# A fused attention and FFN kernel: rounded and low parts side by side in one 512-column product, a moved write-out and a new repeated order

## The chip, the cores and the metric

The kernel runs on one core of one Trainium2 chip. The metric is the device time of an execution in microseconds. A core has TensorE (PE in the rows; PEld is its weight load), VectorE (DVE), ScalarE (ACT), GpSimd (POOL) and SyncE (SP, which here only issues DMAs). Each engine takes its own instructions in the order in which they stand, and waits for the others through semaphores.

## The reference

Attention with four sink columns and a window of 128 over 4 batches, 8 heads, 768 positions and a head size of 64; its output, laid out as 3072 tokens of 512, goes through an FFN of width 2048 with a hard swish between the layers.

```python
def _attn_ref(q, k, v, n_sink, window):
    scores = (1.0 / np.sqrt(D)) * np.matmul(q, k.transpose(0, 1, 3, 2))
    keep = (pos[None, :] < n_sink) | ((rel >= 0) & (rel < window))   # rel = query - key
    scores = np.where(keep, scores, -1000000000.0)
    a = np.exp(scores - np.max(scores, axis=-1, keepdims=True))
    a = a / (np.sum(a, axis=-1, keepdims=True) + 1e-09)
    return np.matmul(a, v)

def _moe_ref(x, w_in, w_out):          # x (3072, 512), w_in (512, 2048), w_out (2048, 512)
    h = x @ w_in
    g = h * np.clip(h + 3.0, 0.0, 6.0) / 6.0
    return g @ w_out
```

## The kernel before

**Two parts of a number.** An operand is split into a part rounded to the shorter format fp32r and the low part, the difference to the full number. A product then takes three matmuls: rounded x rounded, rounded x low, low x rounded. In the code the names end in h (rounded, high) and l (low): xh, xl, WIH, WIL, gh, g.

**Units and pairs.** The work is cut into 12 units: 4 batches of 3 stretches of 256 positions. A unit has 4 pairs of heads, so there are 48 pairs (s). The first stretches of all batches come first (pairs 0 to 15); the first 10 pairs compute attention in plain fp32.

**Attention of a pair.** `C_score` makes the scores of a head and a tile of 128 queries (c); VectorE reduces them to the row minimum while it writes them to SBUF. `C_soft` does the exponentials (ScalarE), sum and reciprocal (VectorE), an addition of two key blocks (GpSimd) and the scaling (ScalarE, line 331). `D_pt` (d) transposes the weights on TensorE and splits them into ph and pl; GpSimd masks them. `D_snk` (s) does the sink columns. `E_av` (e) multiplies with the values: a head has seven matmuls of 128 or 256 columns, the low ones with 64 output rows. Both heads share one PSUM bank, av. `E_out` joins the two halves in tmp (one ScalarE copy and one VectorE addition a head) and splits the result into xh and xl.

**FFN of a unit.** `ffn1` computes one half (128 of 256 columns of width) of step i: for each of 4 chunks three matmuls of 256 columns, into one half of the bank hps, 12 in all. After both halves ScalarE makes relu(h + 3), VectorE makes min(..., 6) * h, rounds it to gh and takes the low part g. `ffn2` adds that step's share of the second layer for one tile of 128 tokens: six matmuls of 512 columns into o0 or o1. There are 8 steps i; for units from the third on (lag 2) the second layer runs two steps behind the first. `ffn_out` multiplies by 1/6 into SBUF and starts the DMA to the output.

**Order of the work.** A unit's FFN is a queue of 34 places: 16 halves of ffn1, 16 of ffn2 and 2 write-outs. The order in which all instructions are issued is written by hand: a long list for pairs 0 to 15 (FIRST), and then ORDER, repeated for each s; an f in it takes the next place from the FFN queues (`drain`). What remains of the FFN after the last pair is drained at the end. A tile framework puts in the semaphores and gives out the buffers; an instruction whose buffer is still in use is placed later than it is written.

Of the kernel before, what the change touches and what calls it, by code (L numbers as in the profile page):

```python
# [9 lines left out]
F32 = mybir.dt.float32  # L10
# [34 lines left out]
def attn_ffn_kernel(ctx: ExitStack, tc: tile.TileContext, qx, kx, vx, vfx, vsx, n_sink, window, w_in, w_out, out):  # L45
# [248 lines left out]
    PTAGS = [("pl", 2), ("pl", 2), ("Pt", 1)]  # L294

    def cell(s, h, t, c0, c1):

        if plain(s):
            return st_[s][f"P{h}"][:, t * P + c0:t * P + c1]
        return st_[s]["P"][:, h, t * WP + c0:t * WP + c1]  # L300

    def C_score(s, h, t):
# [62 lines left out]
    def D_pt(s, h):  # L365
# [39 lines left out]
    def E_av(s, h):  # L405
# [3 lines left out]
        if h == 0:  # L409
            d["av"] = ps.tile([P, 2, UT], F32, tag="bank", name="av")  # L410
            if not plain(s):
                d["tmp"] = work.tile([P, UT], F32, name="tmp", bufs=1)
        acc = d["av"][:, h, :]

# [4 lines left out]
        if plain(s):  # L419
            pf = d[f"pt{h}"]  # L420
            seq = [(VS[:, slot, h, :], pf[:, c:c + o1 - o0], d["av"][:, 0, o0:o1]) for slot, c, o0, o1 in ops]
        else:

            ph, pl = d[f"pt{h}"]
            vsl = slice(2 * D * h, 2 * D * (h + 1))
            vhi = slice(2 * D * h, 2 * D * h + D)
            high = [(VS[:, slot, vsl], ph[:, c:c + o1 - o0], acc[:, o0:o1]) for slot, c, o0, o1 in ops]
            low = [(VS[:, slot, vhi], pl[:, c:c + o1 - o0], acc[0:D, o0:o1]) for slot, c, o0, o1 in ops]
            seq = [high[0]]
            for a, l in zip(high[1:], low[1:]):  # L430
                seq += [a, l]

            if u:
                seq += [low[0], (sinks[b % 2][:, p, vsl], pz, acc)]
            else:
                seq.append((VS[:, 0, vsl], pl[:, 0:UT], acc))
        for j, (l, r, o) in enumerate(seq):
            nc.tensor.matmul(out=o, lhsT=l, rhs=r, start=(j == 0 and (h == 0 or not plain(s))),
                             stop=(j == len(seq) - 1 and (h == 1 or not plain(s))))
        if h == 1:  # L440
            E_out(s)

    def E_out(s):
        b, u, p = pus[s]
        d = st_[s]
        if p == 0:
            xt[(b, u)] = [None] * NP
        xh = work.tile([P, UT], F32R, tag=f"xh{p}", name=f"xh{p}")
        xl = work.tile([P, UT], F32R, tag=f"xl{p}", name=f"xl{p}")
        xt[(b, u)][p] = (xh, xl)  # L450
        if plain(s):
            acc = d["av"][:, 0, :]
            copy_r(nc, weng(XHF, p), xh, acc)
            nc.vector.tensor_tensor(out=xl, in0=acc, in1=xh.bitcast(F32), op=ALU.subtract)
            return
        tmp = d["tmp"]
        for h, r0, r1 in ((0, slice(0, 64), slice(64, 128)), (1, slice(64, 128), slice(0, 64))):
            acc = d["av"][:, h, :]
            nc.scalar.copy(out=tmp[r0], in_=acc[r1])
            nc.vector.tensor_tensor(out=tmp[r0], in0=acc[r0], in1=tmp[r0], op=ALU.add)  # L460
        copy_r(nc, eng(XHI, s), xh, tmp)
        eng(XLO, s).tensor_tensor(out=xl, in0=tmp, in1=xh.bitcast(F32), op=ALU.subtract)
# [4 lines left out]

    def ffn1(x, i, pool, psum, half, state, tag):

        if half == 0:  # L470
            state["h"] = psum.tile([P, 2, UT], F32, tag=tag or "hps", name="hps")
        hp = state["h"]
        fs = slice(P * half, P * (half + 1))
        n = 3 * NP
        j = 0
        for c in range(NP):
            xh, xl = x[c]
            for l, r in ((WIH[i][:, c, fs], xh), (WIH[i][:, c, fs], xl), (WIL[i][:, c, fs], xh)):
                nc.tensor.matmul(out=hp[:, half, :], lhsT=l, rhs=r, start=(j == 0), stop=(j == n - 1))  # L479
                j += 1  # L480
        if half == 1:
            spare = state["lag"] == 2 and i % 3 == 2
            g = pool.tile([P, 2, UT], F32R, tag="gf" if spare else "g", name="g", bufs=2)
            gh = pool.tile([P, 2, UT], F32R, tag="gf" if spare else "gh", name="gh", bufs=2)
            if state["lag"] == 2:
# [23 lines left out]
    def ffn_out(tt, pool, state, dst):  # L509
        if pool is work:  # L510
            if "o" not in kept:
                kept["o"] = work.tile([P, 2, DM], F32, tag="sb1", name="ost", bufs=1)
            o = kept["o"][:, tt]
# [5 lines left out]
    def ffn_steps(n, x, pool, psum_h, psum_o, dsts, tag=None):  # L519
# [3 lines left out]
        steps = []  # L523
        for i in range(NFP + lag):
# [3 lines left out]
            if i >= lag:  # L528
                for tt in range(2):
                    steps.append((2 * (i - lag + 1), lambda i=i, tt=tt: ffn2(i - lag, tt, psum_o, state, tag)))  # L530
        steps.append((0, lambda: ffn_out(0, pool, state, dsts[0])))
        steps.append((0, lambda: ffn_out(1, pool, state, dsts[1])))
# [267 lines left out]
```

## Time and profile before

| what | value |
|---|---|
| runs shown | 718.99, 717.37, 716.12 us, median 717.37 |
| profiled execution | 716.19 us, its span 714.5 us, granted clock 0.999 |
| TensorE busy | 703.5 us, 4836 matmuls |
| TensorE's weight loads | 640.3 us |
| VectorE busy | 496.0 us |
| ScalarE busy | 413.3 us |
| GpSimd busy | 173.2 us |
| DMA | 89.11 MB, mean 125 GB/s |

The span runs from the first instruction to the last; 1.7 us of the execution's time lie around it. Matmuls overlap: one is printed with some 0.28 or 0.39 us, while the next starts after a shorter time, so what a matmul costs a full TensorE is read from start to start. In the first 170 us the weights are loaded and split, from 170 to 590 the repeated order runs, and from 590 on little but FFN work is left.

### The profile page before, as it was taken

What the parts mean: (1) busy time and instruction counts of PE and PEld (TensorE: products, weight loads), DVE (VectorE), ACT (ScalarE), POOL (GpSimd) and SP (SyncE); (2) the same over time, 40 slices, a digit from 0 to 9 for tenths busy, and PEclk for the clock granted to TensorE, in tenths of its full rate; (3) what the DMA queues carried; (4) which work ended last, traced back from release to release, by engine and by line L of the source; (5) the groups of instructions that cost most, each with busy time, mean ns of one, the idle gap of its engine ahead of it and who ended that gap; (6) DMA issues with size and microseconds to landing.
All of it is one profiled execution on the core that took longest, in us unless ns stands there. A gap on an engine that the chain in (4) does not pass through costs nothing. (4 is left out here: it accounts for less than half of the span.)

```text
span 714.5 us, 14315 instructions
## 1 busy us (share of the span) xinstructions
PE 703.5 (98%) x4836; PEld 640.3 (90%) x4836; DVE 496.0 (69%) x1376; ACT 413.3 (58%) x1080; POOL 173.2 (24%) x336
## 2 busy tenths in 40 slices
PE   9999999999999999999999999999999999999996
PEld 7888888899999999999998998999999899998995
DVE  5999998767777767776777767767776775533331
ACT  6988887676656556556566655655665663311211
POOL 1000000000343333343343343343334344000000
PEclk9999999999999999999999999999999999999999
DMA  8765564555544635545444544553644540000000
GB/s 301 245 216 219 190 198 119 149 132 150 135 103 136 156 103 153 154 104 155 129 111 126 158 111 110 135 150 92 175 129 111 137 99 2 31 1 0 30 1 35
DMA packets 53297, 89.11 MB, mean 125 GB/s; under 512 B 8160, under 2 KB 38112, under 8 KB 51168
## 3 DMA queue, kind: packets, MB, share of 16 engines
q1 hardware_dynamic: 53072, 88.11, 43.6%
q8 instruction: 41, 0.67, 0.4%
q14 instruction: 40, 0.33, 0.1%
q10 hardware_dynamic: 144, 0.00, 0.0%
HBM read 42.47 MB, written 6.29 MB: 68 GB/s over the span
## 5 line engine op out<-in xcount | busy, mean ns | idle before, releaser
L479 PE MATMUL hps<-xh,wih 128*128 128x256 f32 x768 | 219.2, 286 | 0.3 <-DVE tmp L460 0.3
L479 PE MATMUL hps<-xh,wil 128*128 128x256 f32 x768 | 216.6, 282 | 0.0
L479 PE MATMUL hps<-xl,wih 128*128 128x256 f32 x768 | 215.9, 281 | 0.0
L505 PE MATMUL o<-woh,gh 128*128 128x512 f32 x384 | 154.2, 402 | 1.5 <-DVE gh L41 1.5
L505 PE MATMUL o<-woh,g 128*128 128x512 f32 x384 | 151.4, 395 | 0.0
L505 PE MATMUL o<-wol,gh 128*128 128x512 f32 x384 | 151.3, 394 | 0.0
L479 PEld LDWEIGHTS hps<-xh,wih 128*128 128x128 f32 x768 | 144.6, 188 | 2.0 <-PE sp L321 0.5
L479 PEld LDWEIGHTS hps<-xl,wih 128*128 128x128 f32 x768 | 144.8, 188 | 1.2
L479 PEld LDWEIGHTS hps<-xh,wil 128*128 128x128 f32 x768 | 144.6, 188 | 0.1
L492 DVE SCALAR_TENSOR_TENSOR gf<-gf,hps 128x512 f32<-128x512 f32 x96 | 65.7, 685 | 92.8 <-ACT gf L491 92.6
L353 POOL TENSOR_TENSOR Pt<-Pt 128x256 f32<-128x256 f32 x64 | 47.4, 741 | 281.5 <-ACT Pt L345 281.4
L345 ACT ACTIVATE Pt<-Pt,nb 128x272 f32<-128x272 f32 (+2 forms) x152 | 76.9, 506 | 63.3 <-DVE nb L323 62.5
L491 ACT ACTIVATE gf<-hps,three 128x512 f32<-128x512 f32 x96 | 65.9, 687 | 81.2 <-PE hps L479 80.2
L331 ACT ACTIVATE Pt<-Pt,rc 128x144 f32<-128x144 f32 (+2 forms) x152 | 55.3, 414 | 60.4 <-DVE rc L348 36.4
L505 PEld LDWEIGHTS o<-woh,g 128*128 128x128 f32 x384 | 72.2, 188 | 17.3 <-issue 0.3
L505 PEld LDWEIGHTS o<-woh,gh 128*128 128x128 f32 x384 | 72.3, 188 | 11.8 <-ACT gf L491 1.9
L505 PEld LDWEIGHTS o<-wol,gh 128*128 128x128 f32 x384 | 72.4, 189 | 10.3
L494 DVE TENSOR_TENSOR g<-gf,gh 128x512 fp32r<-128x512 f32 x96 | 69.8, 727 | 1.1
L321 PE MATMUL sp<-K 128*128 128x272 f32 (+2 forms) x304 | 60.8, 288 | 1.1 <-DVE pl L30 0.5
L323 DVE CUSTOM_DVE_ANT_0 Pt<-sp,m_t 128x272 f32<-128x272 f32 x128 | 53.8, 428 | 8.3 <-PE sp L321 8.0
L389 POOL TENSOR_SCALAR_AFFINE_SELECT ph<-ph 128x256 fp32r<-128x256 f32 x64 | 30.6, 478 | 117.2 <-ACT ph L35 117.2
L321 PEld LDWEIGHTS sp<-K 128*128 128x128 f32 x304 | 50.3, 188 | 7.8 <-DVE pl L30 0.7
(94 smaller groups left out, 1082.8 us busy)
## 6 DMA issues: line engine op xcount, KB each, us to landing
K<-kt SPq DMA_DIRECT2D x128, 200.0 KB, 3.5
K<-kt SPq DMA_DIRECT2D x152, 64.0 KB, 2.5
st<-in_w_in_dram SPq DMA_DIRECT2D x8, 1024.0 KB, 5.2
st<-in_w_out_dram SPq DMA_DIRECT2D x8, 1024.0 KB, 5.1
kr<-in_kx_dram SPq DMA_DIRECT2D x32, 200.0 KB, 2.4
qr<-in_qx_dram SPq DMA_DIRECT2D x48, 128.0 KB, 2.3
out_dram<-ost SPq DMA_DIRECT2D x24, 256.0 KB, 2.2
vr<-in_vx_dram SPq DMA_DIRECT2D x32, 192.0 KB, 2.5
```

What stands on the lines that cost most here:

```text
L321: nc.tensor.matmul(out=sp[:, 0:w], lhsT=Q[:, h, t * P:(t + 1) * P], rhs=K[:, h, part, k0c:k0c + w], start=(part == 0), stop=(part == 1))
L323: d["min"] = nc.vector.tensor_tensor_reduce(out=cell(s, h, t, 0, w), in0=sp[:, 0:w], in1=m[:, 0:w], scale=-SCALE, scalar=3.0e38, op0=ALU.a ...
L331: nc.scalar.mul(out=blk, in_=blk, mul=c)
L345: d["exp"] = nc.scalar.activation(out=blk, in_=blk, func=AF.Exp, scale=-1.0, bias=nb[:, i:i + 1], accum_out=sm[:, i:i + 1])
L353: nc.gpsimd.tensor_tensor(out=both, in0=both, in1=prior, op=ALU.add)
L389: nc.gpsimd.affine_select(out=prior[i], in_=own[i], pattern=[[0, 2], [-1, P]], base=0, channel_multiplier=1, compare_op=ALU.is_gt, fill=0.0)
L479: nc.tensor.matmul(out=hp[:, half, :], lhsT=l, rhs=r, start=(j == 0), stop=(j == n - 1))
L491: nc.scalar.activation(out=gf, in_=hp, func=AF.Relu, bias=three, scale=1.0)
L492: nc.vector.scalar_tensor_tensor(out=gf, in0=gf, scalar=6.0, in1=hp, op0=ALU.min, op1=ALU.mult)
L494: eng(GLO, state["n"] * NP).tensor_tensor(out=g, in0=gf, in1=gh.bitcast(F32), op=ALU.subtract)
L505: nc.tensor.matmul(out=acc, lhsT=l[:, f, ts_], rhs=r[i][:, f, :], start=(i == 0 and f == 0 and j == 0), stop=(i == NFP - 1 and f == 1 and ...
```

## The change

`ffn1` (units from the third on) multiplies the rounded first-layer weights with xh and xl side by side, as one matmul of 512 columns into both halves of a bank; the low weights still take xh alone. The two results stand beside each other and have to be added: ScalarE copies the second to SBUF (hs), VectorE adds the first. Each half now has a bank of its own, and min and product read h from SBUF. hs lies in the same allocation as the write-out's rows (`spare_rows`, named ost in the rows). `E_av` does the same with ph and pl, in one tile for both, so a head has four matmuls, a bank of its own, and one ScalarE copy and two VectorE additions. Tiles x and ph/pl hold both parts; the plain pairs use one tile for both heads. The write-out is called right after the last `ffn2` of its tile, so a unit's queue has 32 places. ORDER is new.

```diff
-    PTAGS = [("pl", 2), ("pl", 2), ("Pt", 1)]
@@ C_score
-        if t == 0 and plain(s):
-            tag, bufs = PTAGS[(2 * s + h) % len(PTAGS)]
-            d[f"P{h}"] = work.tile([P, 3 * P], F32, tag=tag, name="Ph", bufs=bufs)
+        if i == 0 and plain(s):
+            d["P"] = work.tile([P, 2, 3 * P], F32, tag=("Pt", "ph0")[s % 2], name="Ph", bufs=1)
@@ D_pt
-            ph = work.tile([P, 512], F32, tag="ph", name="pf")
+            if h == 0:
+                d["pf"] = work.tile([P, 2, 512], F32, tag="ph1", name="pf", bufs=1)
+            ph = d["pf"][:, h, :]
...
-        ph = work.tile([P, 512], F32R, name="ph")
-        pl = work.tile([P, 512], F32R, name="pl")
-        d[f"pt{h}"] = (ph, pl)
+        both = work.tile([P, 2, 512], F32R, tag=f"ph{h}", name="ph", bufs=1)
+        ph, pl = both[:, 0, :], both[:, 1, :]
+        d[f"pt{h}"] = both
@@ E_av
-            high = [(VS[:, slot, vsl], ph[:, c:c + o1 - o0], acc[:, o0:o1]) for slot, c, o0, o1 in ops]
-            low = [(VS[:, slot, vhi], pl[:, c:c + o1 - o0], acc[0:D, o0:o1]) for slot, c, o0, o1 in ops]
...
+        av = ps.tile([P, 2, UT], F32, tag="bank", name="av")
+        vsl = slice(2 * D * h, 2 * D * (h + 1))
+        seq = [(VS[:, slot, vsl], d[f"pt{h}"][:, :, c:c + o1 - o0], av[:, :, o0:o1]) for slot, c, o0, o1 in ops]
+        if u:
+            seq.append((sinks[b % 2][:, p, vsl], pz, av[:, 0, :]))
...
+        rows = d["tmp"][D * h:D * (h + 1)]
+        nc.scalar.copy(out=rows, in_=av[D:P, 0, :])
+        nc.vector.tensor_tensor(out=rows, in0=av[0:D, 1, :], in1=rows, op=ALU.add)
+        nc.vector.tensor_tensor(out=rows, in0=av[0:D, 0, :], in1=rows, op=ALU.add)
@@ ffn1
+    def spare_rows():
+        if "sb1" not in kept:
+            kept["sb1"] = work.tile([P, 4, DM], F32, tag="sb1", name="ost", bufs=1)
+        return kept["sb1"]
...
-        for c in range(NP):
-            xh, xl = x[c]
-            for l, r in ((WIH[i][:, c, fs], xh), (WIH[i][:, c, fs], xl), (WIL[i][:, c, fs], xh)):
-                nc.tensor.matmul(out=hp[:, half, :], lhsT=l, rhs=r, start=(j == 0), stop=(j == n - 1))
+        lag2 = state["lag"] == 2
+        if lag2:
+            hp = psum.tile([P, 2, UT], F32, tag=tag, name="hps")
+            for c in range(NP):
+                nc.tensor.matmul(out=hp, lhsT=WIH[i][:, c, fs], rhs=x[c], start=(c == 0), stop=False)
+                nc.tensor.matmul(out=hp[:, 0, :], lhsT=WIL[i][:, c, fs], rhs=x[c][:, 0, :],
+                                 start=False, stop=(c == NP - 1))
+            hs = spare_rows()[:, 2 + i % 2].rearrange("p (a b) -> p a b", a=2)
+            nc.scalar.copy(out=hs[:, half, :], in_=hp[:, 1, :])
+            nc.vector.tensor_tensor(out=hs[:, half, :], in0=hp[:, 0, :], in1=hs[:, half, :], op=ALU.add)
+            hp = hs
@@ ffn_steps
+        def second(i, tt):
+            ffn2(i, tt, psum_o, state, tag)
+            if i == NFP - 1:
+                ffn_out(tt, pool, state, dsts[tt])
...
-        steps.append((0, lambda: ffn_out(0, pool, state, dsts[0])))
-        steps.append((0, lambda: ffn_out(1, pool, state, dsts[1])))
@@ the repeated order
-    ORDER = "v c00 f c01 f c10 f c11 e0 l f k e1 f q f d0 f d1 s f"
+    ORDER = "f f c00 c01 c10 k e0 f q c11 e1 f f l v d0 f f d1 f s"
```

On TensorE, the first two chunks of a half of ffn1, in before (x chunks with their weights, into the bank hps):

```order
L479 MATMUL hps<-xh_4882,wih_110 128x256
L479 MATMUL hps<-xl_4883,wih_110 128x256
L479 MATMUL hps<-xh_4882,wil_118 128x256
L479 MATMUL hps<-xh_5077,wih_110 128x256
L479 MATMUL hps<-xl_5078,wih_110 128x256
L479 MATMUL hps<-xh_5077,wil_118 128x256
```

and the whole half after the change:

```order
L467 MATMUL hps<-x_4754,wih_113 128x512
L468 MATMUL hps<-x_4754,wil_121 128x256
L467 MATMUL hps<-x_4937,wih_113 128x512
L468 MATMUL hps<-x_4937,wil_121 128x256
L467 MATMUL hps<-x_5124,wih_113 128x512
L468 MATMUL hps<-x_5124,wil_121 128x256
L467 MATMUL hps<-x_5313,wih_113 128x512
L468 MATMUL hps<-x_5313,wil_121 128x256
```

Six rows for two chunks became four, with the same number of columns.

On TensorE, the values of one head of a later stretch in before (ph, pl: the two parts of the weights; pz, vs: the sinks):

```order
L438 MATMUL av<-ph,VS 128x256
L438 MATMUL av<-ph,VS 128x128
L438 MATMUL av<-pl,VS 64x128
L438 MATMUL av<-ph,VS 128x128
L438 MATMUL av<-pl,VS 64x128
L438 MATMUL av<-pl,VS 64x256
L438 MATMUL av<-pz,vs 128x256
```

and after the change, with the scores in front of it and the second layer behind it:

```order
L319 MATMUL sp<-K 128x272 x6
L432 MATMUL av<-ph,VS 128x512
L432 MATMUL av<-ph,VS 128x2x128 x2
L432 MATMUL av<-pz,vs 128x256
L507 MATMUL o_5923<-woh_126,gh 128x512
```

Seven matmuls became four, two of which write two runs of 128 columns; and three score groups of two matmuls now stand together ahead of the first head's values.

On VectorE, in before, from a head's scores to the reciprocal of its sums (ISA is the reduction of scores, its second row the read of the minimum; gf, gh and g are the FFN's, sm and rc the sums and reciprocals):

```order
L323 ISA Pt,nb<-sp,m_t_101 128x272
L323 ISA nb 128x1
L323 ISA Pt,nb<-sp,m_t_102 128x272
L323 ISA nb 128x1
L492 SCALAR_TENSOR_TENSOR gf<-gf,hps 128x512
L347 TENSOR_SCALAR sm<-sm 128x2
L41 CAST gh<-gf 128x512
L348 RECIPROCAL rc<-sm 128x2
```

and after the change:

```order
L321 ISA Pt,nb<-sp,m_t_101 128x272
L321 ISA nb 128x1
L494 SCALAR_TENSOR_TENSOR gf<-gf,ost 128x512
L321 ISA Pt,nb<-sp,m_t_102 128x272
L321 ISA nb 128x1
L41 CAST gh<-gf 128x512
L321 ISA Pt,nb<-sp,m_t_101 128x272
L321 ISA nb 128x1
L496 TENSOR_TENSOR g<-gf,gh 128x512
L345 TENSOR_SCALAR sm<-sm 128x2
L435 TENSOR_TENSOR tmp<-av,tmp 64x256
L346 RECIPROCAL rc<-sm 128x2
```

Between the second score and the reciprocal there now stand one more score, the low part g and one of the new value additions.

## Rows read from the trace of the kernel before

**Rows 1.** The page: busy us of each engine; granted clock in 40 slices.
```profile
PE 703.5 (98%) x4836; PEld 640.3 (90%) x4836; DVE 496.0 (69%) x1376; ACT 413.3 (58%) x1080; POOL 173.2 (24%) x336
...
PEclk9999999999999999999999999999999999999999
```

**Rows 2.** Waits of TensorE: engine, line, releaser: us in total, times, longest.
```profile
PE o L505 <- DVE gh L41: 1.5, 1, 1.5
```

**Rows 3.** Timeline of TensorE near the end: start us, us, engine, line, operation.
```profile
608.57 0.34 PE L438 MATMUL av<-ph,VS 128*128 128x256 f32 x2
...
609.22 0.40 PE L505 MATMUL o<-woh,gh 128*128 128x512 f32 x1
...
611.26 0.40 PE L505 MATMUL o<-woh,gh 128*128 128x512 f32 x1
...
618.24 0.28 PE L479 MATMUL hps<-xh,wih 128*128 128x256 f32 x1
...
626.78 0.39 PE L505 MATMUL o<-woh,gh 128*128 128x512 f32 x1
```

**Rows 4.** Windows: stretch, its us, busy us of each engine (instructions), clock, DMA.
```profile
170.00:590.00 420.00, 419.24 (x2944) 385.91 (x2944) 308.91 (x889) 255.36 (x725) 162.92 (x306) 1.00 0.49 128
590.00:714.50 124.50, 118.51 (x757) 106.67 (x755) 45.32 (x97) 23.64 (x48) 7.29 (x15) 1.00 0.04 14
```

**Rows 5.** Groups by form: count | busy us, mean ns of one | idle before.
```profile
L494 DVE TENSOR_TENSOR g<-gf,gh 128x512 fp32r<-128x512 f32 x96 | 69.8, 727 | 1.1
L492 DVE SCALAR_TENSOR_TENSOR gf<-gf,hps 128x512 f32<-128x512 f32 x96 | 65.7, 685 | 92.8 <-ACT gf L491 92.6
L460 DVE TENSOR_TENSOR tmp<-av,tmp 64x256 f32<-64x256 f32 x76 | 31.9, 420 | 13.9 <-ACT tmp L459 13.3
L30 DVE TENSOR_TENSOR pl<-pt,ph 128x256 fp32r<-128x256 f32 x64 | 26.5, 419 | 7.3 <-ACT ph L35 6.2
L35 ACT ACTIVATE ph<-pt 128x256 fp32r<-128x256 f32 x64 | 24.2, 383 | 21.7 <-PE pt L371 21.3
```

**Rows 6.** Timelines of TensorE, VectorE and ScalarE in one repeated pass.
```profile
302.54 0.38 PE L371 MATMUL pt<-ident_r,Pt 128*128 128x128 f32 x2
...
307.60 0.41 PE L321 MATMUL sp<-K 128*128 128x272 f32 x2
307.85 0.39 PE L505 MATMUL o<-woh,gh 128*128 128x512 f32 x1
...
316.67 0.38 PE L371 MATMUL pt<-ident_r,Pt 128*128 128x128 f32 x2
...
305.19 0.42 DVE L30 TENSOR_TENSOR pl<-pt,ph 128x256 fp32r<-128x256 f32 x1
305.52 0.68 DVE L494 TENSOR_TENSOR g<-gf,gh 128x512 fp32r<-128x512 f32 x1
...
309.62 0.69 DVE L492 SCALAR_TENSOR_TENSOR gf<-gf,hps 128x512 f32<-128x512 f32 x1 [1.10 <-ACT gf L491]
...
311.43 0.72 ACT L331 ACTIVATE Pt<-Pt,rc 128x144 f32<-128x144 f32 x2 [1.34 <-DVE rc L348]
```

**Rows 7.** Timeline of TensorE: values of two first-tile heads; split products of a later one.
```profile
130.85 0.41 PE L438 MATMUL av<-ph,VS 128*128 128x256 f32 x2 [0.15 <-DVE gf L492]
...
131.33 0.39 PE L505 MATMUL o<-woh,gh 128*128 128x512 f32 x1
...
313.46 0.28 PE L438 MATMUL av<-ph,VS 128*128 128x128 f32 x1
313.57 0.34 PE L438 MATMUL av<-pl,VS 128*64 128x128 f32 x2
```

**Rows 8.** Timeline of ScalarE at the end of the run.
```profile
707.19 0.60 ACT L516 ACTIVATE ost<-o 128x512 f32<-128x512 f32 x1 [6.33 <-PE o L505]
...
708.59 0.60 ACT L516 ACTIVATE ost<-o 128x512 f32<-128x512 f32 x1 [0.81 <-PEq L646]
```

**Rows 9.** The page, DMA issues: count, KB each, median us to landing.
```profile
K<-kt SPq DMA_DIRECT2D x128, 200.0 KB, 3.5
```

More of the change, by code (lines that the diff above doesn't have):

```diff
@@ L408, in E_av @@
         VS = d["VS"]
[L409 to L413, printed above, removed]
         if u:
@@ L437, in E_av @@
-        for j, (l, r, o) in enumerate(seq):
-            nc.tensor.matmul(out=o, lhsT=l, rhs=r, start=(j == 0 and (h == 0 or not plain(s))),
-                             stop=(j == len(seq) - 1 and (h == 1 or not plain(s))))
+            if h == 0:
+                d["av"] = ps.tile([P, UT], F32, tag="bank", name="av")
+            pf = d["pf"][:, h, :]
+            seq = [(VS[:, slot, h, :], pf[:, c:c + o1 - o0], d["av"][:, o0:o1]) for slot, c, o0, o1 in ops]
+            for j, (l, r, o) in enumerate(seq):
+                nc.tensor.matmul(out=o, lhsT=l, rhs=r, start=(j == 0 and h == 0), stop=(j == len(seq) - 1 and h == 1))
@@ new lines, in E_av @@
+            if h == 1:
+                split_x(s, d["av"])
+            return
+        if h == 0:
+            d["tmp"] = work.tile([P, UT], F32, name="tmp", bufs=1)
+        av = ps.tile([P, 2, UT], F32, tag="bank", name="av")
[3 more added lines that the diff above has]
+            seq.append((sinks[b % 2][:, p, vsl], pz, av[:, 0, :]))
+        for j, (l, r, o) in enumerate(seq):
+            nc.tensor.matmul(out=o, lhsT=l, rhs=r, start=(j == 0), stop=(j == len(seq) - 1))
@@ L440, in E_av, with split_x @@
+        rows = d["tmp"][D * h:D * (h + 1)]
+        nc.scalar.copy(out=rows, in_=av[D:P, 0, :])
+        nc.vector.tensor_tensor(out=rows, in0=av[0:D, 1, :], in1=rows, op=ALU.add)
+        nc.vector.tensor_tensor(out=rows, in0=av[0:D, 0, :], in1=rows, op=ALU.add)
         if h == 1:
-            E_out(s)
-    def E_out(s):
+            split_x(s, d["tmp"])
+    def split_x(s, src):
         b, u, p = pus[s]
-        d = st_[s]
         if p == 0:
             xt[(b, u)] = [None] * NP
[L448 to L462, printed above, removed]
@@ L465, in attn_ffn_kernel @@
+        xb = work.tile([P, 2, UT], F32R, tag=f"x{p}", name=f"x{p}")
+        xt[(b, u)][p] = xb
+        hi, lo = (weng(XHF, p), nc.vector) if plain(s) else (eng(XHI, s), eng(XLO, s))
+        copy_r(nc, hi, xb[:, 0, :], src)
+        lo.tensor_tensor(out=xb[:, 1, :], in0=src, in1=xb[:, 0, :].bitcast(F32), op=ALU.subtract)
     LAG2 = 2
     kept = {}
+    def spare_rows():
+        if "sb1" not in kept:
+            kept["sb1"] = work.tile([P, 4, DM], F32, tag="sb1", name="ost", bufs=1)
+        return kept["sb1"]
@@ new lines, in ffn1 @@
+        if lag2:
[8 more added lines that the diff above has]
+            hp = hs
+        else:
+            if half == 0:
+                state["h"] = psum.tile([P, 2, UT], F32, tag=tag or "hps", name="hps")
+            hp = state["h"]
+            for c in range(NP):
+                xh, xl = x[c][:, 0, :], x[c][:, 1, :]
+                for j, (l, r) in enumerate(((WIH, xh), (WIH, xl), (WIL, xh))):
+                    nc.tensor.matmul(out=hp[:, half, :], lhsT=l[i][:, c, fs], rhs=r,
+                                     start=(c == 0 and j == 0), stop=(c == NP - 1 and j == 2))
@@ L510, in ffn_out @@
         if pool is work:
-            if "o" not in kept:
-                kept["o"] = work.tile([P, 2, DM], F32, tag="sb1", name="ost", bufs=1)
-            o = kept["o"][:, tt]
+            o = spare_rows()[:, tt]
         else:
```

34 lines of the change are left out of this document (7 added, 27 removed).

## The prediction

> **What bounds the kernel now.** I read the page's busy table first, then the waits of TensorE, its timeline for the spacing of products, the windows, and last the chain of one softmax. TensorE is busy for 703.5 of 714.5 us, at full granted clock (the 2.4 GHz level) in all 40 slices [rows 1]. Ends of matmuls are modelled, so that share alone proves little; the waits do: the longest total of its own is 1.5 us, a single wait [rows 2]. TensorE is fed, and the time is the sum of what its products occupy. What one occupies is the distance from its start to the next start, not its printed duration. In the FFN work near the end, 30 products of 512 columns stand between 611.26 and 618.24 (0.2327 us each) and 72 of 256 columns between 618.24 and 626.78 (0.1186 each) [rows 3]. Two of 256 take 0.2372, which is 0.0045 us more than one of 512: columns cost nearly the same, an instruction a few ns. That is the whole lever of the first half of this change.
>
> VectorE is busy for 308.9 and ScalarE for 255.4 of the 420 us from 170 to 590, the stretch of repeated passes (74% and 61%); from 590 on both are mostly idle [rows 4].
>
> **The change part by part.**
>
> *First layer of the FFN.* Ten of the twelve units (from the third on) are altered. Each has 8 steps of 2 halves with 4 chunks, so 640 pairs of 256-column products become one product of 512; the product with the low weights stays. 640 x 0.0045 = 2.9 us off TensorE. The ends I keep are 0 (a pair costs what the wide one does) and 5 us (8 ns a pair).
>
> Added: 160 copies of 128x256 out of PSUM on ScalarE and 160 additions of 128x256 on VectorE. The nearest rows are the ScalarE copy of 128x256 from PSUM, 383 ns, and the VectorE subtraction of 128x256 with one operand in PSUM, 419 ns [rows 5]; I take these: 61 us on ScalarE, 67 us on VectorE in all. From below, a VectorE operation of this size holds up the next one for 0.33 us only (305.19 to 305.52 [rows 6]), which makes 53 us; from above stand the 685 ns of an operation of twice the columns [rows 5], 110 us. The product min(...)*h now reads its second operand in SBUF instead of PSUM: between the 685 ns it takes now and the 727 ns of the low part of g, which has both in SBUF [rows 5]; at 80 calls at most 3 us of VectorE. None of this is on TensorE; what hides it is worked out below.
>
> *Values.* A head of a later tile pair had seven products, from 608.57 to 609.22, 0.65 us [rows 3]. It now has one of 512 columns and three of 256: 0.2327 + 3 x 0.1186 = 0.589. So 0.061 less, for 64 heads 3.9 us. The twelve heads of first tiles that are not in plain fp32 go from four products to two, 0.351 us by the same spacing; before, four of them lie between 130.85 and 131.33, 0.48 us, behind a wait of 0.15 [rows 7]: 0 to 0.13 saved, I take 0.06, 0.7 us in all. Two of the four new products of such a head, and one of the two of a first tile, write two runs of 128 columns with a gap between. No product of before shows that. From below they cost what 256 columns cost, 0.119; from above, what two products of 128 columns cost, up to 0.11 each (313.46 to 313.57 [rows 7]), so 0.22. I take 0.119, since the column count is the same; the upper end is 140 x 0.10 = 14 us.
>
> On this the Trainium skill speaks against the change: its page "PSUM — Partial Sum Buffer", Specifications (TRN2), says that any non-contiguous access pattern slows matmuls significantly, with lines of 8 bytes. No row here shows such a write; each run of these is 512 bytes long, which is why the rule gets a small chance below.
>
> VectorE gets 76 more additions of 64x256 at 420 ns [rows 5], 32 us.
>
> *Write-out.* The two write-out steps of a unit were places in the queue without a product; now the same ScalarE multiply and DMA follow the unit's last products. At the end of the run nothing moves: the first half's multiply already starts at 707.19, beside the other half's products, and the last one at 708.59 behind the last product [rows 8]. Each of the eight FFN places of a pass now carries products, so attention is spread over more FFN work and the tail gets shorter: a shift, zero in the sum.
>
> *New order.* Three of the four score groups and the first value group stand together, and FFN steps in pairs. Neither has a price on TensorE in the old passes. The keys' step stands one score earlier, but its DMAs write the single K buffer, so they are still held until the fourth score has read it; the larger of them take 3.5 us to land [rows 9], and the next pass's first score comes some 11 us after that score. SP's loads behind them are for later passes. Zero, and if that cover were gone the wait would show as TensorE waiting on DMA.
>
> *Buffers of the plain start.* The first ten pairs share fewer buffers; the written-out start is otherwise the same. Zero, 2 us either way.
>
> **Sum.** 2.9 + 3.9 + 0.7 = 7.5 us. The profiled execution has a span of 714.5 and a time of 716.19, so 1.7 lie around it; its new time would be 708.7. The median of the runs shown, 717.37, lies 1.2 above it and would become 709.9. I say 709.
>
> **What hides the additions.** A pass (one pair of heads) lasts 14.1 us on TensorE, from the transposes at 302.54 to those at 316.67 [rows 6]. VectorE at 74% has some 10.4 us in it. It gains four FFN additions and two value additions, 2.5 us by durations, 2.0 by starts: 12.4 to 12.9 of 14.0 us, and 1.1 to 1.6 us are left. ScalarE goes from 8.6 to 10.1. Capacity is there; the question is the order of arrival. In before, from the second score (307.60) to the end of the scaled weights (311.43 + 0.72 = 312.15) the softmax of a head takes 4.55 us, and its transposes come at 316.67 only [rows 6]. In the new order there stand between them two scores of 0.25 (307.60 to 307.85), two value groups of 0.59, one second-layer step and two first-layer halves of 1.40 each: 5.9 us, with the second score's own 0.25 6.1. VectorE's queue now holds one more score, one low part of g and one value addition ahead of the reciprocal: 0.43 + 0.73 + 0.42 by durations, about 1.3 us by starts. If all of that adds, the chain takes 5.85 of 6.1 us; but in the old chain VectorE was idle for 1.10 us before its product at 309.62 [rows 6], and part of the added work falls in there. So the slack is 0.25 to 1.5 us: enough, but here the change can fail.
>
> **Rivals.**
>
> A, forecast: TensorE stays the bound and saves its 7.5 us. Its own range is 705 to 713. Chance 0.62.
>
> B, the other side: the scaled weights of the first head come too late, the transposes wait in each of the 32 full passes, and as TensorE takes its products in order, the FFN products queued behind wait with them. For it: VectorE at 88 to 92%, and that slack. Against it: the idle 1.10 us; and the second layer runs two steps behind the first, so it has several us before it needs g. It decides from 0.23 us a pass (7.5 / 32), where the gain is gone; at 0.5 us a pass the time is 709 + 16 = 725. Chance 0.11.
>
> C, the same wait at about 0.25 us a pass, or in some passes only: 709 + 8 = 717, no change. Chance 0.15.
>
> D, the split writes of the values cost as two products each: 709 + 14 = 723. Chance 0.05. This is what the rule of the Trainium skill's PSUM page would do here.
>
> E, the wide product gives nothing, since a column costs the same in either form: only the values gain, 4.6 us, 712. For it: the difference is 4.5 ns in 237. Chance 0.07. On this the Trainium skill's page "TensorE: Matmul & The Clock Gate", Back-to-back issue gap, gives N/2.4 + 2.5 ns per product, so an estimate of 2.5 ns a pair and 1.6 us in all; its sustained 131 ns for 512 columns in the same section does not fit this trace, which has 232.7.
>
> **Numbers.** A measurement of this kernel can tell about 0.5% from no change: 713.8 to 721.0 is the same. Faster: A and most of E, 0.68. Same: C and a little of E and B, 0.18. Slower: the rest of B and D, 0.14. The range is 704 to 718: it holds A, C and E, and B and D lie above it.
>
> **What would show it.** In the profile after: a first-layer half with eight products in 1.40 us instead of 1.42; a head's values in 0.59. VectorE busy near 595 us and ScalarE near 475, where the page of before has 496 and 413 [rows 1]. Starts of the products with two runs 0.12 apart confirm the price, 0.2 is D. Waits of TensorE that stay under some 3 us in total say A; a wait of the transposes on ScalarE that comes back in each pass says B or C. The forecast is wrong if the products' spacing shrinks as said but the sum of TensorE's waits grows by 7 us or more.

## The result, and the profile after

The changed kernel takes 708.16 us (median of 4 runs, 706.12 to 709.82), the kernel before 716.75 beside it (median of 4). The ratio is 0.9877, 95% interval [0.9834, 0.992]; a second set of runs (below) gave 0.9892 [0.9869, 0.9915]. The forecast was 709 in 704 to 718. The profiled execution took 709.82 us, its span 708.1.

The page of after, busy us of each engine:

```profile
PE 695.5 (98%) x3980; PEld 601.0 (85%) x3980; DVE 578.7 (82%) x1612; ACT 474.2 (67%) x1240; POOL 197.1 (28%) x336
```

TensorE has 856 matmuls fewer than in [rows 1] (640 pairs, 64 x 3 in the values of later tiles, 12 x 2 of first tiles). VectorE and ScalarE carry the new work, and GpSimd, whose instructions are the same, takes 24 us more.

Windows of after (the columns of [rows 4]):

```profile
170.00:590.00 420.00, 420.00 (x2326) 362.51 (x2325) 371.27 (x1065) 299.05 (x834) 177.79 (x291) 1.00 0.49 126
590.00:708.10 118.10, 112.12 (x573) 94.22 (x572) 65.53 (x161) 45.24 (x112) 16.38 (x29) 1.00 0.11 33
```

In the repeated passes VectorE went from 74% to 88%, and TensorE still has no gap: 420.00 of 420.00 us. Its own waits, the three largest by total:

```profile
PE pt L369 <- ACT Ph L329: 2.3, 1, 2.3
PE idle L86 <- POOL rel L65: 1.2, 1, 1.2
PE o L507 <- DVE gh L41: 1.1, 1, 1.1
```

Each is one single wait, as in [rows 2], and none lies between 190 and 600 us, where no product and no weight load of TensorE waits for `Pt`, the weights of later pairs. Spacing of products, timeline of TensorE in after:

```profile
613.07 0.63 PE L432 MATMUL av<-ph,VS 128*128 128x512 f32 x3
613.53 0.28 PE L432 MATMUL av<-pz,vs 128*128 128x256 f32 x1
613.65 0.39 PE L467 MATMUL hps<-x,wih 128*128 128x512 f32 x1
...
657.20 0.40 PE L467 MATMUL hps<-x,wih 128*128 128x512 f32 x1
...
665.61 0.39 PE L507 MATMUL o<-woh,gh 128*128 128x512 f32 x1
```

A head's values take 0.58 (613.07 to 613.65), where [rows 3] had 0.65. Six halves of the first layer with 48 products stand between 657.20 and 665.61: 1.402 each, where the 72 products of [rows 3] took 1.423.

One pass of after, from sink product to sink product, with the softmax that can stop it (TensorE, then ScalarE):

```profile
400.57 0.22 PE L400 MATMUL spt<-ident_r,ssc 128*128 128x128 f32 x1
...
409.90 0.38 PE L369 MATMUL pt<-ident_r,Pt 128*128 128x128 f32 x2
...
414.52 0.22 PE L400 MATMUL spt<-ident_r,ssc 128*128 128x128 f32 x1
...
408.93 0.72 ACT L329 ACTIVATE Pt<-Pt,rc 128x144 f32<-128x144 f32 x2 [0.65 <-DVE rc L346]
```

The pass lasts 13.95 us (14.13 in [rows 6]). The scaled weights end at 409.65, and their transposes start at 409.90: a slack of 0.25 us by this measure, the lower end of what was forecast.

**Pass lengths.** A pass can be read to 0.05 us from the start of one sink product to the next, far finer than the time of a run: two profiled executions of the changed kernel whose spans are 2.5 us apart both have a mean of 13.922. This table is worked out from those starts, 31 passes in each kernel, the mean without the first three and the last two:

```
kernel                                       usual pass      longer ones                     mean
changed                                      13.87 to 13.95  none but the last (14.35)       13.92
old first layer                              13.95 to 14.11  none                            14.02
new order and write-out alone                14.05 to 14.20  none                            14.12
old order                                    13.85 to 13.95  3 of 14.04 to 14.08             13.89
old values, joined together                  14.01 to 14.04  22 of 14.59 to 14.92            14.59
old values, joined head by head              14.00 to 14.04  14 of 14.31 to 15.14            14.31
 the same, row minimum ahead of the product  13.99 to 14.11  4 of 14.21 to 14.33             14.07
low part of g twice                          -               13.95 to 15.08, 23 of 14.4 on    14.62
transposes together                          13.88 to 13.93  7 of 14.54 to 14.62, last 14.40 14.09
 the same, first values later                13.88 to 13.93  none                            13.90
```

### The profile page after: what moved, and what is told of

The parts are those of the page before. It is cut to its first block, busy times and chain, and to the rows that moved or that the text cites. A ratio compares the mean times of both kernels' runs of the same rounds, so it can differ in the third digit from the quotient of the medians.

```text
span 708.1 us, 13020 instructions
## 1 busy us (share of the span) xinstructions
PE 695.5 (98%) x3980; PEld 601.0 (85%) x3980; DVE 578.7 (82%) x1612; ACT 474.2 (67%) x1240; POOL 197.1 (28%) x336
## 4 chain that ended last, share of the span: by engine, by line
PE 89%; DMA 3%; ACT 3%; DVE 2%; SPq 1%; issue 1%; ACTq 0%; DVEq 0%
PE o L507 36%; PE hps L467 21%; PE hps L468 11%; PE av L432 6%; PE sp L319 5%; PE hps L481 4%; PE pt L369 3%; DMA st<-in_w_in_dram 2%; PE av L419 1%; PE idle L86 1%; PE sp L314 1%; SPq L271 1%; DMA K<-kt 1%; DMA raw<-in_n_sink_dram 1%; ACT st L163 1%
## 5 line engine op out<-in xcount | busy, mean ns | idle before, releaser
L467 PE MATMUL hps<-x,wih 128*128 128x512 f32 x640 | 233.3, 400 | 0.0
L468 PE MATMUL hps<-x,wil 128*128 128x256 f32 x640 | 180.4, 282 | 0.0
L351 POOL TENSOR_TENSOR Pt<-Pt 128x256 f32<-128x256 f32 x64 | 57.6, 900 | 345.7 <-ACT Pt L343 345.7
L467 PEld LDWEIGHTS hps<-x,wih 128*128 128x128 f32 x640 | 120.5, 188 | 23.3
L468 PEld LDWEIGHTS hps<-x,wil 128*128 128x128 f32 x640 | 120.7, 189 | 0.4
L493 ACT ACTIVATE gf<-ost,three 128x512 f32<-128x512 f32 x80 | 57.8, 723 | 61.4 <-DVE ost L472 61.4
L471 ACT COPY ost<-hps 128x256 f32<-128x256 f32 x160 | 58.1, 369 | 57.8 <-PE hps L468 56.1
L472 DVE TENSOR_TENSOR ost<-hps,ost 128x256 f32<-128x256 f32 x160 | 66.5, 416 | 31.8 <-ACT ost L471 31.3
L389 POOL TENSOR_SCALAR_AFFINE_SELECT ph<-ph 128x256 fp32r<-128x256 f32 x128 | 74.0, 579 | 53.9 <-ACT ph L35 53.9
L507 PEld LDWEIGHTS o<-woh,gh 128*128 128x128 f32 x384 | 72.4, 188 | 14.7 <-ACT gf L493 1.4
L507 PEld LDWEIGHTS o<-wol,gh 128*128 128x128 f32 x384 | 72.6, 189 | 11.9
L494 DVE SCALAR_TENSOR_TENSOR gf<-gf,ost 128x512 f32<-128x512 f32 x80 | 55.7, 697 | 22.2 <-ACT gf L493 19.6
L391 POOL TENSOR_SCALAR_AFFINE_SELECT ph<-ph 128x256 fp32r<-128x256 f32 x128 | 66.5, 522 | 26.1 <-DVE ph L30 18.5
```

Of the source, the lines that this page charges most:

```text
L351: nc.gpsimd.tensor_tensor(out=both, in0=both, in1=prior, op=ALU.add)
L389: nc.gpsimd.affine_select(out=prior[i], in_=own[i], pattern=[[0, 2], [-1, P]], base=0, channel_multiplier=1, compare_op=ALU.is_gt, fill=0.0)
L391: nc.gpsimd.affine_select(out=own[i], in_=own[i], pattern=[[0, 2], [1, P]], base=0, channel_multiplier=-1, compare_op=ALU.is_ge, fill=0.0)
L467: nc.tensor.matmul(out=hp, lhsT=WIH[i][:, c, fs], rhs=x[c], start=(c == 0), stop=False)
L468: nc.tensor.matmul(out=hp[:, 0, :], lhsT=WIL[i][:, c, fs], rhs=x[c][:, 0, :], start=False, stop=(c == NP - 1))
L471: nc.scalar.copy(out=hs[:, half, :], in_=hp[:, 1, :])
```

## The experiments

Theory: TensorE stays fed, and the gain is the sum of smaller products. Rivals: the new order or the write-out made it; the softmax's slack is used up; VectorE's total, not its order, is what limits.

**The changed kernel again.** No edit.

> The changed kernel once more, on the chip and beside the runs of the next three. Every theory: a ratio to before of 0.986 to 0.991.

708.29 us (704.96 to 712.30, 6 runs), ratio 0.9892 [0.9869, 0.9915]. The gain holds in a second set of runs. The runs scatter over 7 us, those of before beside them over 3 (714.35 to 717.32, 17 runs); more on that below.

**Old first layer.** Three products of 256 columns a chunk, no additions.

```
-        if lag2:
+        if False:
             hp = psum.tile([P, 2, UT], F32, tag=tag, name="hps")
```

> The changed kernel with its first layer as before (three products of 256 columns a chunk into one bank for both halves, no copy and no addition), the rest changed. Theory (the gain is the sum of fewer products on TensorE): 2.9 to 3.8 us slower than the changed kernel, so a ratio to before of about 0.992; first-layer halves 1.42 us instead of 1.40; VectorE busy falls by some 67 us and that gains nothing. Rival (the gain is the new order and write-out, the products are worth nothing): the ratio stays at 0.988. Rival (the additions on VectorE cost time): faster than the changed kernel, ratio under 0.986.

709.51 us (708.02 to 710.57), 0.9916 [0.9903, 0.9929]. Its passes are 0.097 us longer than those of the changed kernel, 3.0 us over 31 passes. By the ratio alone (0.0024 apart, intervals that overlap) the first layer's part would not be told from nothing; by the pass it is.

**New order and joined write-out alone,** on the kernel before.

```
-    ORDER = "v c00 f c01 f c10 f c11 e0 l f k e1 f q f d0 f d1 s f"
+    ORDER = "f f c00 c01 c10 k e0 f q c11 e1 f f l v d0 f f d1 f s"
...
+        def second(i, tt):
+            ffn2(i, tt, psum_o, state, tag)
+            if i == NFP - 1:
+                ffn_out(tt, pool, state, dsts[tt])
```

> The kernel before with only the new repeated order and the write-out joined to the last step; products as before. Theory: 0 on TensorE, ratio 0.998 to 1.002. Rival (the gain is order and write-out): 0.988 to 0.992.

713.43 us (12 runs), 0.9978 [0.9969, 0.9987]: 1.6 us, a small gain and not quite zero. In before TensorE's products wait three times between 190 and 600 us (twice for keys, `K<-kt`, 0.5 us in all, once 0.3 us for the joining); here none does. From here to the old first layer only the values (and buffers) differ: 0.097 us a pass again.

**Old order** in the changed kernel (the ORDER line above, the other way round).

> The changed kernel with the old repeated order. Theory: the order is worth nothing on TensorE as long as it is fed; the old order leaves the first head more time between its scores and its transposes but packs the second one closer, so a ratio of 0.988 to 0.991 to before and waits of TensorE under 5 us more. Rival (the added work on VectorE is only hidden because of the new order): TensorE waits for scores or transposes in each pass, 0.3 us or more a pass, ratio 1.0 or above.

708.77 us, 0.991 [0.9896, 0.9925], against 0.9892 with the new order: no difference that can be told, and its passes are no longer (13.89 against 13.92). The order is not what made the gain.

**Old values.** Seven products a head, both heads in one bank, joined after the second.

```
+            d["av"] = ps.tile([P, 2, UT], F32, tag="bank", name="av")
...
+        for x, l in zip(high[1:], low[1:]):
+            seq += [x, l]
...
+            for g, r0, r1 in ((0, slice(0, 64), slice(64, 128)), (1, slice(64, 128), slice(0, 64))):
+                nc.scalar.copy(out=d["tmp"][r0], in_=acc[r1])
+                nc.vector.tensor_tensor(out=d["tmp"][r0], in0=acc[r0], in1=d["tmp"][r0], op=ALU.add)
```

> The changed kernel with the values' products as before (seven a head, one bank for both heads, one addition a head), the rest changed. Theory: 4.6 us slower than the changed kernel, ratio to before about 0.994; a head's values 0.65 us instead of 0.59; VectorE busy some 32 us less. Rival (order and write-out): 0.988. Rival (VectorE's additions cost time): under 0.986.

729.23 us, 1.0199 [1.0176, 1.0222]: the forecast of 0.994 failed by 18 us. Only some passes have the 14.02 us that the products add up to. VectorE had less to do (340.7 us of the 420) than in the changed kernel (371.3), so it isn't its total. TensorE's weight loads wait between 190 and 600 us for the softmax and, less, for GpSimd's masks:

```profile
PEld pt L369 <- ACT Pt L329: 10.7, 26, 0.8
PEld av L441 <- POOL ph L391: 5.3, 7, 0.8
```

**Old values, joined head by head.** The same products, a bank for each head, copy and addition right behind each.

```
+        acc = ps.tile([P, UT], F32, tag="bank", name="av")
...
+        nc.scalar.copy(out=rows, in_=acc[D:P])
+        nc.vector.tensor_tensor(out=rows, in0=acc[0:D], in1=rows, op=ALU.add)
```

> The changed kernel with the values' seven products a head as before, but each head in a bank of its own and joined right after its products, as in the changed kernel (one addition a head instead of two). Theory (the run with the old values lost its time because both heads were joined only after the second, which filled ScalarE and VectorE just ahead of the second softmax, not because of the products): no waits in the passes, 4 to 4.6 us slower than the changed kernel, ratio about 0.994. Rival (the products or the low ones with 64 output rows cost far more in the new order): again 1.01 to 1.02.

720.45 us, 1.0069 [1.0054, 1.0085]. Neither range came (0.994, or 1.01 to 1.02): half of the loss against 0.994 is gone, and 14 of 31 passes are still long. Timelines of the longest, 15.14 us, TensorE, VectorE, ScalarE:

```profile
421.93 0.66 PE L319 MATMUL sp<-K 128*128 128x272 f32 x4
...
429.31 0.62 PE L369 MATMUL pt<-ident_r,Pt 128*128 128x128 f32 x2
429.69 0.48 PE L514 MATMUL o<-woh,gh 128*128 128x512 f32 x1
...
424.11 0.41 DVE L479 TENSOR_TENSOR ost<-hps,ost 128x256 f32<-128x256 f32 x1
425.31 0.69 DVE L501 SCALAR_TENSOR_TENSOR gf<-gf,ost 128x512 f32<-128x512 f32 x1 [0.79 <-ACT gf L500]
425.92 0.43 DVE L321 CUSTOM_DVE_ANT_0 Pt<-sp,m_t 128x272 f32<-128x272 f32 x1
...
428.83 0.72 ACT L329 ACTIVATE Pt<-Pt,rc 128x144 f32<-128x144 f32 x2 [0.17 <-POOL Pt L351]
```

The first score starts at 421.93, and VectorE takes its row minimum at 425.92 only. Right ahead of it stands the FFN product min(...)*h, for which VectorE waits 0.79 us with nothing to do, because its operand comes from ScalarE; wait and product take 1.4 of the 4.0 us, work queued earlier the rest. The scaled weights end at 429.55, and the second transpose waits for them. In the changed kernel the row minimum stands ahead of that product in the same place, 0.9 us behind its score, which starts at 417.4:

```profile
418.34 0.44 DVE L321 CUSTOM_DVE_ANT_0 Pt<-sp,m_t 128x272 f32<-128x272 f32 x1
419.20 0.69 DVE L494 SCALAR_TENSOR_TENSOR gf<-gf,ost 128x512 f32<-128x512 f32 x1 [0.41 <-ACT gf L493]
```

ORDER writes the product first in both kernels: it belongs to the f ahead of c00. In the changed kernel the framework placed it behind the row minimum in every pass but the last, here it kept the written order in most. Why a change in the values moved it is not shown. The place alone doesn't tell a long pass either: 16 short passes have the product first too, and in 7 of the 14 long ones the row minimum comes first. So the next edit, and not this timeline, is the evidence.

**Row minimum ahead of the product,** the two kernels above with this alone altered: min(...)*h, gh and g of a pass's first step are held back.

```
+            if kept.get("hold"):
+                late.append(product)
...
+                if step == "c00":
+                    with tc.issue_after(st_[at]["min"].ins):
+                        for product in late:
+                            product()
```

> The kernel with the values' old seven products, joined head by head (1.0069 before), with one thing altered: in the repeated order VectorE takes the FFN product min(...)*h of the pass's first step only behind the first score's row minimum. In the run without this, passes in which that product (which waits for ScalarE) stood ahead of the row minimum took 14.5 to 15.1 us, and the others 14.02 to 14.04. Theory, VectorE's queue: all passes become 14.0 to 14.1 us, some 8 us less in all, ratio 0.994 to 0.997. Rival, the seven products themselves make the next step late (their bank or GpSimd's masks): passes of 14.5 us and more stay, ratio 1.004 to 1.009.

712.63 us, 0.9962 [0.9941, 0.9984]: the passes fall to a mean of 14.07, as the theory had it, those with the row minimum first among them; four of 14.21 to 14.33 us are left. The sorting of passes in this expectation (product first 14.5 to 15.1 us, the others 14.02 to 14.04) is wrong, as said above; what it forecast came all the same. VectorE in a pass of 14.31 us, at the same place of its unit as the one above:

```profile
307.15 0.41 DVE L480 TENSOR_TENSOR ost<-hps,ost 128x256 f32<-128x256 f32 x1
307.49 0.42 DVE L321 CUSTOM_DVE_ANT_0 Pt<-sp,m_t 128x272 f32<-128x272 f32 x1
...
308.35 0.69 DVE L505 SCALAR_TENSOR_TENSOR gf<-gf,ost 128x512 f32<-128x512 f32 x1 [0.43 <-ACT gf L501]
308.96 0.43 DVE L321 CUSTOM_DVE_ANT_0 Pt<-sp,m_t 128x272 f32<-128x272 f32 x1
```

> The same alteration for the kernel with the old values in one bank for both heads (1.0199 before; passes of 14.02 us and of 14.6 to 14.9). Theory, VectorE's queue: the transposes' waits go, passes near 14.05 us, ratio 0.994 to 0.998; where GpSimd's masks stay late for the values behind the old joining of both heads, up to 1.005. Rival, the shared bank or the joining of both heads behind the second head is what makes the passes long: they stay, ratio 1.015 or more.

727.52 us, 1.0172 [1.0152, 1.0192]: here the rival holds. With both heads joined behind the second one, 22 passes stay long whichever stands first, and in them VectorE takes the first row minimum some 4.8 to 5.5 us into the pass (3.5 to 4.4 in the changed kernel). So there are two causes: how the heads are joined (1.0172 against 0.9962; the shared bank and the later joining are not told apart), and the place of one step's FFN work in VectorE's queue (1.0069 against 0.9962).

**Low part of g twice.** VectorE takes the low part of g a second time, 1.2 us more a pass.

```
+            if lag2:
+                eng(GLO, state["n"] * NP).tensor_tensor(out=g, in0=gf, in1=gh.bitcast(F32), op=ALU.subtract)
```

> The changed kernel with the low part g computed twice in the units from the third on: two more VectorE operations of 0.7 us a pass, 0.6 us each from start to start. VectorE has about 1.6 us idle in a pass of 13.9. Theory (the slack of the first head's softmax, 0.3 us in the tightest passes of the trace, is the limit, not VectorE's capacity): TensorE waits for the transposes, 0.2 to 0.6 us in some passes, 5 to 20 us in all, ratio 0.995 to 1.015. Rival (capacity is the limit): 1.2 of 1.6 us fit, ratio as the changed kernel's, 0.986 to 0.991.

728.69 us, 1.0183 [1.0168, 1.0198]. VectorE is busy for 393.9 of 420 us and has room left, yet the time grows by 20 us, 0.70 a pass, a little more than the theory's range. The waits between 190 and 600 us stand with TensorE's weight load, since the transposed block is what it loads:

```profile
PEld pt L369 <- ACT Pt L329: 23.0, 69, 0.9
```

This is the mechanism of the prediction's rival B: 1.2 us more in VectorE's queue, counted by starts, meet a slack of 0.20 to 1.18 us, and what the slack does not take is paid, in some passes more and in some less (13.95 to 15.08 us).

**Transposes together.** Both heads' transposes at the end of the pass, one switch less on TensorE.

```
+    ORDER = "f f c00 c01 c10 k e0 f q c11 e1 f f l v f f d0 d1 f s"
```

> The changed kernel with the transposes of the two heads one behind the other (the step d0 moved behind the next two FFN steps). In the trace of the changed kernel the product behind a pair of transposes starts 0.31 us later instead of 0.23, twice a pass; once of it goes. Theory: 0.083 us x 32 passes, 2.7 us faster than the changed kernel, ratio about 0.984, and more slack for the first head. Rival (GpSimd's masks of both heads then come in one block and the next pass's values wait for them): waits of the values on GpSimd, ratio 0.99 or above.

711.65 us (12 runs), 0.9957 [0.9943, 0.9971]: slower than the changed kernel, where 0.984 was expected. The only waits of TensorE's products between 190 and 600 us, and one of them:

```profile
PE av L432 <- POOL ph L391: 2.8, 7, 0.4
...
305.17 0.74 PE L432 MATMUL av<-ph,VS 128*128 128x512 f32 x3 [0.41 <-POOL ph L391]
```

Every fourth pass the first head's values wait for GpSimd's masks, the first of which now starts 1.2 to 2.6 us later in the pass. The switch saved hardly brings anything: the passes without a wait are 13.88 to 13.93 us, 0.02 less in the mean than the changed kernel's, where 0.083 was expected.

**The same, first values one step later.**

```
+    ORDER = "f f c00 c01 c10 k f e0 q c11 e1 f f l v f f d0 d1 f s"
```

> The changed kernel with both heads' transposes together at the end of the pass (0.9957 before, passes of 13.88 to 13.92 us and every fourth one of 14.54 to 14.62, in which the first head's values waited for GpSimd's masks), and with the first head's values one FFN step later in the next pass. Theory, GpSimd's masks are what made that fourth pass long: it falls to 13.9 us, 0.65 us x 8 = 5 us less, ratio 0.987 to 0.990, no more than the changed kernel gains. Rival, the values' lateness moves on to their joining and the softmax behind it on VectorE and ScalarE: some passes of 14.3 us and more stay, ratio 0.993 to 0.998.

708.51 us (705.10 to 713.28), 0.9921 [0.9891, 0.9951]. The long passes are gone (all 13.88 to 13.93), so the masks were their cause. The ratio lies above the 0.987 to 0.990 of the theory, but the interval is too wide to rank this kernel beside the changed one, and a pass 0.02 us shorter is worth 0.7 us.

**Weights behind the first attention.** ScalarE's first copy of FFN weights, which waits for a DMA, behind the first pair's scaling.

```
+            d["copied"] = copy_r(nc, {"D": nc.vector, "A": nc.scalar}[PFE[h]], ph[:, 0:w], pt[:, 0:w])
...
+                if after == 0:
+                    behind.enter_context(tc.issue_after(st_[0]["copied"].ins))
```

> The changed kernel with one thing altered in its start: ScalarE takes its first copy of FFN weights, which waits for a DMA, only behind the first pair's scaling and copies. In two profiled executions of the changed kernel (spans 708.1 and 710.6 us) that copy waited 2.72 us for the DMA, TensorE then waited 2.3 and 2.1 us for the scaling queued behind it, and the granted clock fell to 0.71 and 0.50 for the next 5 us; in the execution of 703.4 us of the variant with the transposes together the copy waited 1.10 us and the clock stayed at 1.00. Theory, this one wait with the clock that follows it is the scatter of the changed kernel's times (705 to 712 us): the runs gather near 705, ratio 0.985 to 0.988, the clock at 1.00 from 10 to 20 us. Rival, the start is late in some executions for other transfers too (the keys' and queries' loads): the wait moves, the scatter and the median stay, ratio 0.988 to 0.992.

711.11 us (708.42 to 712.54), 0.9939 [0.9921, 0.9956]. The wait and the low clock between 10 and 20 us are gone, as the theory had it, but TensorE then stood idle in other places of the start (3.73 of 5 us busy from 15 to 20, 3.39 from 30 to 35), and the median grew, above both forecasts. The theory that this one wait is the scatter falls.

## Why the prediction was right, and where it was off

**What bounds.** TensorE was full before and stays full. The sum of all distances from one product's start to the next went from 706.9 to 700.5 us in the two profiled executions: first layer 277.9 to 275.4, values 60.0 to 56.3; the rest cancels (the new order and the start, both below, are in it).

**The sum, a pass.** The prediction's prices make 16 x 0.0045 + 2 x 0.061 = 0.194 us a pass. From new order and write-out alone to the whole change the mean pass falls from 14.12 to 13.92, 0.194. That the two agree so closely is luck. By the starts of the products, in the same 26 passes, the values go from 1.295 to 1.173 us when they (and the buffers) change, 0.122 as priced, and the first layer from 5.846 to 5.735 when it follows, 0.111 where 0.072 was forecast; at each step the rest of the pass takes a little longer, 0.04 in all, and 0.097 are left of each. In the FFN work near the end a pair saves 5.4 ns ((8.54 - 8.41) / 24), where 4.5 was taken, the same lever slightly larger; so rival E, that the wide product is worth nothing, is out. By the estimate from the Trainium skill's page "TensorE: Matmul & The Clock Gate", Back-to-back issue gap, a pair would save 2.5 ns; the rows show twice that.

**Split writes (rival D).** The distance from a product with two runs of 128 columns to the next is 0.118 us (median of 140), the low end of the bound; in the rows above, one product of 512 columns and two of these take 0.46. The Trainium skill's page "PSUM — Partial Sum Buffer", Specifications (TRN2), would have such a write slow the matmul significantly; no row here shows it, with runs of 512 bytes.

**The additions.** Rows of after, groups by form:

```profile
L472 DVE TENSOR_TENSOR ost<-hps,ost 128x256 f32<-128x256 f32 x160 | 66.5, 416 | 31.8 <-ACT ost L471 31.3
...
L471 ACT COPY ost<-hps 128x256 f32<-128x256 f32 x160 | 58.1, 369 | 57.8 <-PE hps L468 56.1
L351 POOL TENSOR_TENSOR Pt<-Pt 128x256 f32<-128x256 f32 x64 | 57.6, 900 | 345.7 <-ACT Pt L343 345.7
L494 DVE SCALAR_TENSOR_TENSOR gf<-gf,ost 128x512 f32<-128x512 f32 x80 | 55.7, 697 | 22.2 <-ACT gf L493 19.6
```

416 and 369 ns, where 419 and 383 were taken from [rows 5]; ScalarE's 474.2 us are the forecast's 475. VectorE's 578.7 are less than the 595: the added durations do sum to 97 us, but the page counts an overlap of two instructions once, and VectorE starts one 0.08 us before the last ends. The estimate by starts was the better of the two. The product min(...)*h, 697 ns, lies between its bounds of 685 and 727.

**The slack (rivals B and C).** Forecast 0.25 to 1.5 us (with 1.10 us of idle time in the old chain it should have been 1.35 at most), found 0.20 to 1.18 by the same measure, from the end of a first head's scaled weights to its transposes. The first transpose needs only the first of the two blocks that are scaled: where transposes wait, in the run with the low part twice, they start 0.25 us ahead of the end of the second, so the tightest passes had some 0.45 us to spare. It held in 30 of 31 passes. In the last, 14.35 us long, the second head's transposes waited; the wait stands with the weight load:

```profile
621.88 0.14 PEld L369 LDWEIGHTS pt<-ident_r,Pt 128*128 128x128 f32 x1 [0.46 <-ACT Pt L329]
```

That B and C were real is shown by the neighbours: the old values, the low part taken twice, the transposes together each lose 3 to 21 us by waits for the softmax or the masks. A chance of 0.26 for the two was not too much.

**Write-out and order** were taken as 0: together 1.6 us, a gain, from waits of before that the prediction had read as too short to count: three of its passes took 14.3 to 14.7 us where the usual ones take 14.04 to 14.20, and one of those with two write-out places in place of products 11.9 where the others take 11.2 to 11.4. Order and write-out were not tried apart. At the end nothing moved, as forecast: the last two multiplies start 1.41 us apart, in [rows 8] 1.40. The keys' loads hid, as forecast.

**The start** was the term with the poorest ground (0, 2 us either way). Windows of after and of before from 10 to 20 us, and the wait ahead of the low clock (ScalarE, TensorE; of before ScalarE's copy alone):

```profile
10.00:15.00 5.00, 2.66 (x13) 1.55 (x14) 1.30 (x8) 3.15 (x9) 0.00 (x0) 0.95 1.00 415
15.00:20.00 5.00, 5.00 (x31) 4.57 (x29) 3.08 (x9) 3.27 (x8) 0.00 (x0) 0.71 0.45 154
...
11.85 1.12 ACT L159 ACTIVATE wt<-st 128x1024 f32<-128x1024 f32 x1 [2.72 <-DMA st<-in_w_in_dram]
12.87 0.50 ACT L329 ACTIVATE Ph<-Ph,rc 128x256 f32<-128x256 f32 x1
...
13.42 0.44 PE L369 MATMUL pt<-ident_r,Ph 128*128 128x128 f32 x2 [2.34 <-ACT Ph L329]
```

```profile
10.00:15.00 5.00, 4.72 (x34) 3.60 (x34) 2.80 (x16) 4.70 (x13) 0.00 (x0) 1.00 1.00 411
15.00:20.00 5.00, 5.00 (x37) 4.11 (x36) 4.59 (x14) 4.93 (x12) 0.00 (x0) 1.00 0.63 205
...
10.30 1.13 ACT L159 ACTIVATE wt<-st 128x1024 f32<-128x1024 f32 x1 [0.90 <-DMA st<-in_w_in_dram]
```

In this execution of after the first weights land later, ScalarE holds the first pair's scaling back behind them, TensorE idles for 2.3 us, and then its granted clock is 0.71 in the mean of 5 us, part of the time its lower level (1.2 GHz). Another execution of it had 0.50 there. The first sink product of the repeated order starts at 191.87 and 194.19 us in these two; in the fastest profiled execution, of the kernel with the first values one step later, which has the same work up to there, it starts at 188.24. So 3.6 and 5.9 us were lost, more than the 2 us that the prediction allowed. The mean granted clock of the changed kernel's ten runs is 0.993 to 1.000, that of the 17 runs of before beside them 0.997 to 0.999. So some 4 to 6 us of the gain are lost in some executions and not in others: the fastest run is 704.96, the slowest 712.30. Which part of the change lets it happen stays open. With the old values or the old order the clock of some runs falls to 0.993 as well, and with new order and write-out alone it stayed at 0.997 to 0.999 in 12 runs, so neither the new values nor the new order is needed for it, and order and write-out alone do not bring it. The kernel with the old first layer, which has the same buffers in its start, kept 0.997 to 0.999 in six runs; moving the one copy did not cure it; the buffers alone were not tried.

**The number.** The forecast was 709 and the median 708.16, and that is luck in part. Two terms taken as nothing were not: order and write-out gave 1.6 us, and the start took some 4 to 6 us back in some executions. They act against each other and against a product gain that is a little larger than priced. What is shown is the mechanism: TensorE stays fed, and each pass is shorter by what its products save.

## What to carry to other kernels

Where an engine is full, price a change by the distance from start to start, and check it by the length of one repeated pass: 0.1 us a pass is plain there, while the time of a run hides 3 us in its scatter. When work is put on an engine that is busy for 88%, ask what its queue holds ahead of the chain that the full engine waits for, not whether there is room: 1.2 us a pass cost 20 us with 6% of VectorE still free. And where a framework places the instructions, an edit far off can change which of two comes first on an engine, and put one that waits ahead of one that is waited for; read the order on that engine before and after, and do not take it from the program's text.

## What the runs showed of the hardware

An addition on GpSimd and an operation on VectorE hold each other up: the one that begins second takes longer. VectorE, then GpSimd, in one pass of after:

```profile
309.49 0.69 DVE L496 TENSOR_TENSOR g<-gf,gh 128x512 fp32r<-128x512 f32 x1
310.10 0.71 DVE L345 TENSOR_SCALAR sm<-sm 128x2 f32<-128x2 f32 x1
...
309.61 1.16 POOL L351 TENSOR_TENSOR Pt<-Pt 128x256 f32<-128x256 f32 x1 [2.64 <-ACT Pt L343]
```

Here the subtraction g begins first: it keeps its usual 0.69 us, and the addition takes 1.16. So it is in all 24 passes where it begins 0.12 us behind a g (1.16 to 1.17 us); all the others but one (0.92) take 0.73 to 0.75. In before, the addition began first twice: it took 0.73 and 0.74, and the g beside it 1.25. VectorE's operation on two columns, 0.17 us where it stands alone, begins behind the addition, takes 0.71 and ends with it. Over the run GpSimd's addition went from 0.74 to 0.90 us in the mean, though nothing of its own changed: 10 of the 24 us that GpSimd gained, the masks have the rest. None of it made TensorE wait between 190 and 600 us in the changed kernel.
